# RWKV-5 attention with a SwiGLU block on one core: state update in 32-column groups, and another order of the opening

## The chip, the cores and the metric

The kernel runs on one core of a Trainium2 chip. The metric is device time in microseconds, the median over runs of the same program; lower is better. Timelines count from the start of the profiled span.

## The reference

Inputs are r, k and v of shape (4, 8, 768, 48) (batch, heads, tokens, head width D), w and u of shape (8, 48), and three float32 weights: `w_gate` and `w_val` of 384x1536, `w_out` of 1536x384. First the attention with a decaying state, then the FFN on all 3072 tokens:

```python
for t in range(S):
    kt, vt, rt = k[:, :, t], v[:, :, t], r[:, :, t]
    cur = einsum('bhd,bhe->bhde', u[None] * kt, vt)
    y[:, :, t] = einsum('bhd,bhde->bhe', rt, state + cur)
    state = w[None, :, :, None] * state + einsum('bhd,bhe->bhde', kt, vt)
x = y.transpose(0, 2, 1, 3).reshape(B * S, H * D)
g = x @ w_gate
out = (g * (1 / (1 + exp(-g))) * (x @ w_val)) @ w_out
```

All values are float32.

## The kernel before

**Units.** A unit is one chunk of 128 tokens of one batch entry; there are 24, numbered with the batch innermost, so that unit i is batch i mod 4 and chunk i div 4, and units 0 to 3 have no earlier state. For a unit, `load` fetches k and r (token on the partitions) and `load_v` fetches v. `own_product` (POOL, two multiplies into `rk`) and `own_sum` (DVE, a reduction into `du`) make the product of a token with itself. `scale_k` and `scale_r` (POOL) multiply k and r by powers of w, giving `khat` and `rhat` in slots of the tile `hats`; `turn` transposes them on PE (`tp`) into `kT` and `rT`. For units 0 and 1 the raw k and r are transposed and multiplied by tables of powers (`pw`, `pv`) on DVE as they leave PSUM; from unit 2 on the scaled ones are transposed and copied out by ACT. From unit 12 (`BLOCKS`) DMA and DVE transpose instead.

`diagonal` writes `du` on the diagonal of the 128x128 score tiles `At` (eight heads, two buffers), by ACT one head at a time or by one multiply on POOL or DVE for several heads. `scores` makes kT against rT on PE (`s_ps`), and DVE's `copy_predicated` writes it above the diagonal, half of the heads at a time. `outputs` makes y in 32-column groups on PE: a matmul writes 32 of the 128 PSUM partitions, four groups beside each other; its terms are scores times v and state times r. ACT copies y to `xT`.

**State.** `Z[b]` holds, for each pair of heads, a 112x96 tile in which the two 48x48 blocks on the diagonal are states. `update` adds a unit: one matmul per pair gives both heads against both, and a multiply with `wL`, which is zero off the two blocks, discards the cross terms:

```python
dve.tensor_add(z[0:R2], ps[0:R2], z[0:R2])
pool.tensor_mul(z[0:R2], z[0:R2], w)
```

Units 20 to 23 have no update. `wL` is made from `own`, a mask of two columns, early in the program.

**Weights.** 18 blocks (`chunks`) of 768 elements per partition arrive as pairs of 32-bit words in three buffers and are rounded: ACT makes `w_mag` from the upper words (in two halves, in two PSUM banks) and `w_low` from the lower ones, DVE puts sign and magnitude together (two operations a half, `round_dve`), and POOL adds the low part (`round_pool`). `round_act` does ACT's and DVE's share of a block and starts later loads, `round_weights` does a POOL add for the block ahead and then `round_act`. Four weight sums for `w_out` follow on POOL.

**FFN.** For units 0 to 3, `gate_value` makes a feature block of 128 columns for a pair of units: six matmuls into `gv`, a sigmoid, two DVE multiplies. It stands in a list, `todo`, with the number of rounded blocks that it needs; `feed(n)` takes the first entries that are ready by program order. Later units go in fours (`four`, `project`) with fewer products, spread over the steps in the same way.

**Order.** Each engine runs its instructions in the order in which the program issues them (a schedule by hand), and DMA starts go through SP's queue in order. The opening is written out call by call; then a loop over steps s from 4 calls `own_sum`, `scale`, `own_product`, loads, `turn`, `scores(s - 1)`, `outputs(s - 2)` and `update(s - 2)`, with `gaps(s, n)` between them: each takes a weights step ("R") or an FFN piece ("F") from a table up to step 11, and a share of `todo` after that. From step 12 (`LATE`) on, `outputs` stands right behind `scores`. `warm(n)` puts matmuls of the identity with no use of the result into PE's queue.

Of the kernel before, what the change touches and what calls it, by code (L numbers as in the profile page):

```python
# [15 lines left out]
P = 128  # L16
# [6 lines left out]
def fast(  # L23
# [50 lines left out]
    rscale = cst.tile([P, H, D], FP32, name="rscale")  # L74
    own = cst.tile([P, 2], FP32, name="own")
    wL = cst.tile([P, HP, 2, D], FP32, name="wL")
    w128 = cst.tile([P, HP], FP32, name="w128")
# [29 lines left out]
    def raw(i):  # L107

        if i < 2:
            return khat[i][:, :, 0:D], rhat[i][:, :, 0:D]  # L110
        return k_ld[i % 2][:], r_ld[i % 2][:]
# [57 lines left out]

    def round_act(next_load=1):  # L170
        n = next_chunk("act")
        if n is not None:
            mags[n] = []
            lows[n] = two.tile([P, WN], INT32, name="w_low", tag="w_low")
            for hi, (ps, tag) in zip(halves(bits[n][:, :, 1], n), ((ps_w, "w_mag"), (ps_o, "o"))):
                mag = ps.tile([P, WN // 2], INT32, name="w_mag", tag=tag)
                mags[n].append(mag[:].rearrange("p (c f) -> p c f", c=hi.shape[1]))
                act.activation(  # L178
                    mags[n][-1].bitcast(FP32), hi.bitcast(FP32), AF.Abs, scale=float(2.0**-112)
                )  # L180
                if len(mags[n]) == 1:
                    act.activation(
                        lows[n][:], bits[n][:, :, 0].bitcast(UINT32), AF.Copy, scale=float(2.0**-29)
                    )
                    round_dve(n, 0)
            round_dve(n, 1)
            del bits[n]
            for _ in range(next_load):
                load_weights()

    def round_dve(n, half):
        hi = halves(bits[n][:, :, 1], n)[half]
        f = hi.shape[2]
        dst = chunks[n][1].bitcast(INT32)
        dst = dst[:, :, half * f : half * f + f] if hi.shape[1] == 3 else dst[:, half : half + 1]
        dve.tensor_scalar(dst, hi, -(1 << 31), None, ALU.bitwise_and)  # L196
        dve.scalar_tensor_tensor(  # L197
            dst, mags[n][half], 3, dst, ALU.logical_shift_left, ALU.bitwise_or
        )

    def round_pool():
        n = next_chunk("pool")
        if n is not None:
            del mags[n]
            dst = chunks[n][1].bitcast(INT32)
            low = lows.pop(n)[:].rearrange("p (c f) -> p c f", c=dst.shape[1])
            pool.tensor_tensor(dst, dst, low, ALU.add)
# [8 lines left out]
    def own_product(i):  # L216
        kl, rl = raw(i)
        if i == 1:

            rk = At[1][:, 0:3, :].rearrange("p x t -> p (x t)").rearrange("p (h d) -> p h d", h=H)  # L220
        else:
            rk = one.tile([P, H, D], FP32, name="rk", tag="rk")[:]
        pool.tensor_mul(rk, rl, kl)
        pool.tensor_mul(rk, rk, ub[:])
        rks[i] = rk
# [9 lines left out]
    dve.memset(hats[:, 0:6, :, D:64], 0.0)  # L235
    dve.memset(wcol[:], 1.0)
    for e in range(2):
        sp.dma_start(out=wcol[64 * e : 64 * e + D, :], in_=w.rearrange("(a e) d -> e d a", e=2)[e])
# [13 lines left out]
    def warm(n):  # L252

        ps = ps_f.tile([P, 2, 2 * P], FP32, name="warm", tag="gv")
        for _ in range(n):
            pe.matmul(ps[:, 0, 0:P], ident[:], ident[:], start=True, stop=True)

    warm(18)

    pool.memset(own[:], 1.0)  # L260
    for step, base in ((-64, 0), (64, D - 1)):
        pool.affine_select(
            out=own[:], in_=own[:], compare_op=ALU.is_ge, fill=0.0,
            base=base, pattern=[[step, 2]], channel_multiplier=1 if step < 0 else -1,
        )

# [48 lines left out]
    def diagonal(i):  # L315

        du = dus.pop(i)
        on_act = (HP, 0, H)[min(i, 2)]
        small.extend(
            lambda h=h: act.activation(  # L320
                At[i % 2][:, h, :], ident[:], AF.Identity, scale=du[:, h : h + 1]
            )
            for h in range(on_act)
        )
        if on_act < H:
            n = H - on_act
            (pool if i else dve).tensor_mul(
                At[i][:, on_act:H], ident[:].unsqueeze(1).to_broadcast([P, n, P]),
                du[:, on_act:H].unsqueeze(2).to_broadcast([P, n, P]),
            )  # L330
# [4 lines left out]
    def turn(i):  # L335
        for nm, t, table in (
            ("kT", khat[i % 4], pw[:, :, 1 : P + 1]), ("rT", rhat_of(i), pv)
        ):
            tp = ps_a.tile([P, HP, P], FP32, name="tp", tag="a")
            for a in range(HP):  # L340
                pe.transpose(tp[:, a, :], pair(t, a), ident[:])
            if nm == "kT":
                dst = kT[i % 2]
            else:
                dst = turned[i] = three.tile([P, HP, P], FP32, name=nm, tag=nm)
            if i < 2:
                dve.tensor_mul(dst[:], tp[:], table)
# [71 lines left out]
    def update(i):  # L419
# [3 lines left out]
        kh, vl, z = khat[i % 4], v_ld[i % 4], Z[b]  # L423
        ps = ps_a.tile([P, HP, D2], FP32, name="u_ps", tag="a")
        for a in range(HP):
            pe.matmul(  # L426
                ps[0:R2, a, :].rearrange("p (e d) -> p e d", e=2),
                pair(kh, a)[:, 0:R2],
                bass.AP(
                    tensor=vl.tensor, offset=vl[:, a, 0:1].offset,  # L430
                    ap=[list(vl[:].ap[0]), [64, 2], [1, D]],
                ),
                start=True, stop=True, skip_group_check=True,
            )
        w = wL[0:R2].rearrange("p a e d -> p a (e d)")
        if c == 0:
            dve.tensor_mul(z[0:R2], ps[0:R2], w)
        else:
            dve.tensor_add(z[0:R2], ps[0:R2], z[0:R2])
            pool.tensor_mul(z[0:R2], z[0:R2], w)  # L440

# [245 lines left out]
    def queue(g):  # L687
        if g == 0:
            todo.extend(
                (2 * f2 + 2, lambda j=j, f=f: gate_value(j, f))  # L690
                for f2 in range(FC // 2) for j in range(2) for f in (2 * f2, 2 * f2 + 1)
# [32 lines left out]
    EARLY[4] = ("R", "F", "", "F", "F")  # L724


    turn(0)
    natural_tables()
    own_sum(0)
    diagonal(0)  # L730
    own_product(1)
    load(2)
    load_v(2)
    load_weights()
    load(3)
    load_v(3)
    warm(3)
    turn(1)
    while small:
        small.popleft()()  # L740
    own_sum(1)
    scale_k(0)
    diagonal(1)
    scores(0)
    round_act(0)
    scores(1)
    warm(3)
    scale_k(1)
    outputs(0)
    round_pool()  # L750
    round_act()
    scale(2)
    outputs(1)
    round_pool()
    dve.tensor_copy(w128[:].unsqueeze(2), pw[:, :, 0:1])
    dve.tensor_mul(
        wL[:], w128[:].unsqueeze(2).unsqueeze(3).to_broadcast([P, HP, 2, D]),
        own[:].unsqueeze(1).unsqueeze(3).to_broadcast([P, HP, 2, D]),
    )

    dve.tensor_tensor(bad[:], held[:], wcol[:], ALU.not_equal)
    dve.tensor_reduce(badc[:], bad[:], axis=AX.X, op=ALU.add)
    dve.memset(ones[:], 1.0)

    own_product(2)
    scale(3)
    warm(4)
    queue(0)
    round_act(2)
    load(4)  # L770
    turn(2)
    own_product(3)
    update(0)
    update(1)
    own_sum(2)
    diagonal(2)
    feed(1, 8)
    turn(3)
    round_act(0)
    own_sum(3)  # L780
    scores(2)
    round_pool()
    load_v(4)
    load(5)
    feed(1)
    diagonal(3)
    while small:
        small.popleft()()
    scores(3)
    outputs(2)  # L790
    update(2)
    round_pool()
    scale(4)
    outputs(3)
    load_weights()
    update(3)
    round_act()
    own_product(4)
    load(6)
    feed(2)  # L800
    own_sum(4)
    round_weights()
    for s in range(4, N + 2):
# [11 lines left out]
        if 4 <= s - 1 < N:  # L815
# [3 lines left out]
            if s >= LATE:  # L819
                outputs(s - 2)  # L820
            gaps(s, 1)
        if BLOCKS <= s < N:
# [4 lines left out]
        if s - 2 >= 4 and (s < LATE or s > N):  # L827
            outputs(s - 2)
        if s >= 5 and s % 2:
            queue((s - 3) // 2)  # L830
        if s < N:
            diagonal(s)
        if s - 2 >= 4:
            gaps(s, 3)
            update(s - 2)
        gaps(s, 4)
        if s == 12:
            n_ps = ps_a.tile([P, HP, P], FP32, name="n_ps", tag="a")
            pe.matmul(n_ps[0:1, 0, 0:1], badc[:], ones[:], start=True, stop=True)
# [418 lines left out]
```

## Time and profile before

| | |
|---|---|
| median of three runs | 640.49 us (639.94 to 641.51) |
| profiled execution | 640.14 us, span 638.3 us |
| TensorE clock granted, mean | 0.995 |
| busy: PE / DVE / POOL / ACT | 624.0 / 367.4 / 299.1 / 242.0 us |
| DMA | 40.40 MB, mean 63 GB/s |
| PE, state update (`u_ps`) | 160 records for 80 matmuls |
| DVE, state (L437, L439) | 4 and 16 operations, median 552 and 557 ns |
| POOL, state (L440) | 16 operations, median 1000 ns |

A matmul is pipelined, so that its recorded duration is longer than the time until the next one can start: the distance between starts is its price when PE is full. A float32 matmul leaves two records. The weight loads of the array have a row of their own (PEld) and run beside matmuls. A row of a timeline has its start, its length, the engine, the line, the operation, and the tiles written and read; in brackets stands the engine's idle time before it and what ended that.

### The profile page before, as it was taken

What the parts mean: (1) busy time and instruction counts of PE and PEld (TensorE: products, weight loads), DVE (VectorE), ACT (ScalarE), POOL (GpSimd) and SP (SyncE); (2) the same over time, 40 slices, a digit from 0 to 9 for tenths busy, and PEclk for the clock granted to TensorE, in tenths of its full rate; (3) what the DMA queues carried; (4) which work ended last, traced back from release to release, by engine and by line L of the source; (5) the groups of instructions that cost most, each with busy time, mean ns of one, the idle gap of its engine ahead of it and who ended that gap; (6) DMA issues with size and microseconds to landing.
All of it is one profiled execution on the core that took longest, in us unless ns stands there. A gap on an engine that the chain in (4) does not pass through costs nothing.

```text
span 638.3 us, 11992 instructions
## 1 busy us (share of the span) xinstructions
PE 624.0 (98%) x4570; PEld 561.6 (88%) x4570; DVE 367.4 (58%) x729; ACT 242.0 (38%) x655; POOL 299.1 (47%) x330
## 2 busy tenths in 40 slices
PE   8889999999999999999999999999999999999996
PEld 8678888899888889988899988889988889988896
DVE  7859998455356565366558255666255545355460
ACT  3558776421343421244431234442243320234310
POOL 5868877934837431754534734631432311444110
PEclk9989999999999999999999999999999999999998
DMA  8969873233322113212221402021100000000001
GB/s 197 263 161 232 223 213 89 40 65 73 79 48 37 33 26 71 66 32 52 45 47 31 109 5 46 16 40 27 51 1 2 1 1 26 26 1 1 2 2 53
DMA packets 138003, 40.40 MB, mean 63 GB/s; under 512 B 128592, under 2 KB 131792, under 8 KB 137936
## 3 DMA queue, kind: packets, MB, share of 16 engines
q1 hardware_dynamic: 134480, 34.82, 24.8%
q10 hardware_dynamic: 3456, 4.72, 2.1%
q8 instruction: 38, 0.62, 0.4%
q14 instruction: 29, 0.24, 0.1%
HBM read 28.51 MB, written 4.72 MB: 52 GB/s over the span
## 4 chain that ended last, share of the span: by engine, by line
PE 85%; DVE 8%; ACT 3%; POOL 1%; issue 1%; DMA 0%; SPq 0%; DVEq 0%; ACTq 0%
PE c_b L628 24%; PE c_a L628 20%; PE o_f L522 13%; PE o_a L522 8%; PE o_b L522 6%; PE y_ps L413 5%; PE gv L451 4%; PE s_ps L383 3%; PE u_ps L426 2%; ACT At L320 1%; DVE wg L196 1%; DVE At L388 1%; DVE wv L196 1%; ACT w_mag L178 1%; DVE wv L197 1%
## 5 line engine op out<-in xcount | busy, mean ns | idle before, releaser
L612 POOL TENSOR_TENSOR hT<-hT,u 128x256 f32<-128x256 f32 x60 | 47.5, 792 | 161.2 <-DVE hT L611 134.2
L635 ACT COPY u<-c_a 128x256 f32<-128x256 f32 x120 | 44.5, 371 | 86.9 <-PE c_a L628 85.6
L628 PE MATMUL c_a<-t,wv 128*128 128x256 f32 x240 | 72.2, 382 | 0.1
L628 PE MATMUL c_b<-xT,wg 128*128 128x256 f32 x240 | 71.7, 380 | 0.0
L608 ACT ACTIVATE sg<-hT 128x256 f32<-128x256 f32 x120 | 50.0, 416 | 54.2 <-DVE hT L637 35.5
L320 ACT ACTIVATE At<-ident,du 128x128 f32<-128x128 f32 x180 | 63.0, 398 | 12.5 <-DVE o_sb L536 7.8
L628 PE MATMUL c_b<-xT,s 128*128 128x256 f32 x240 | 61.6, 379 | 0.0
L642 DVE TENSOR_TENSOR u<-u,c_b 128x256 f32<-128x256 f32 x60 | 25.1, 418 | 62.1 <-PE c_b L628 55.1
L628 PEld LDWEIGHTS c_b<-xT,s 128*128 128x128 f32 x240 | 45.3, 190 | 6.6 <-DVE u L642 0.2
L628 PEld LDWEIGHTS c_a<-t,wv 128*128 128x128 f32 x240 | 44.7, 190 | 7.0 <-ACT u L635 1.1
L628 PEld LDWEIGHTS c_b<-xT,wg 128*128 128x128 f32 x240 | 45.2, 190 | 6.2 <-issue 0.4
L588 POOL TENSOR_TENSOR s<-wv,wg 128x256 f32<-128x256 f32 x24 | 17.8, 741 | 69.8 <-PE o_f L522 55.3
L637 DVE TENSOR_TENSOR hT<-p,c_b 128x256 f32<-128x256 f32 x60 | 25.2, 419 | 43.5 <-PE c_b L628 40.0
L388 DVE COPY_PREDICATED At<-mask,s_ps 128x512 f32<-128x512 int32 x48 | 32.8, 739 | 18.1 <-PE s_ps L383 10.8
L413 PE MATMUL y_ps<-At,v_ld 128*32 128x128 f32 x768 | 36.1, 279 | 4.7 <-DVE At L388 4.7
L451 PE MATMUL gv<-xT,wg 128*128 128x256 f32 x144 | 36.8, 391 | 0.0
L644 DVE TENSOR_TENSOR hT<-u,c_b 128x256 f32<-128x256 f32 x60 | 25.2, 421 | 19.4 <-PE c_b L628 19.2
L413 PEld LDWEIGHTS y_ps<-At,v_ld 128*32 128x32 f32 x768 | 30.9, 112 | 6.1 <-DVE At L388 5.7
L628 PE MATMUL c_b<-t,s 128*128 128x256 f32 x120 | 36.2, 383 | 0.0
L640 DVE TENSOR_TENSOR hT<-hT,c_a 128x256 f32<-128x256 f32 x60 | 25.3, 421 | 18.9 <-PE c_a L628 17.5
L628 PE MATMUL c_b<-xT,wv 128*128 128x256 f32 x120 | 35.9, 381 | 0.0
L628 PE MATMUL c_a<-xT,wg 128*128 128x256 f32 x120 | 35.8, 380 | 0.0
(139 smaller groups left out, 1411.7 us busy)
## 6 DMA issues: line engine op xcount, KB each, us to landing
hats<-hats SPq DMA_DIRECT2D x192, 32.0 KB, 1.9
w_bits<-in_moe_w_gate_dram SPq DMA_DIRECT2D x6, 768.0 KB, 5.9
v_ld<-in_v_dram SPq DMA_DIRECT2D x48, 96.0 KB, 3.0
w_bits<-in_moe_w_val_dram SPq DMA_DIRECT2D x6, 768.0 KB, 5.8
w_bits<-in_moe_w_out_dram SPq DMA_DIRECT2D x6, 768.0 KB, 5.1
out_dram<-o_sb ACTq DMA_DIRECT2D x24, 192.0 KB, 1.9
k_ld<-in_k_dram SPq DMA_DIRECT2D x22, 192.0 KB, 2.8
r_ld<-in_r_dram SPq DMA_DIRECT2D x22, 192.0 KB, 3.7
```

Of the source, the lines that this page charges most:

```text
L320: lambda h=h: act.activation(At[i % 2][:, h, :], ident[:], AF.Identity, scale=du[:, h : h + 1])
L388: dve.copy_predicated(At[i % 2][:].rearrange("p (a e) t -> p a e t", e=2)[:, :, e], mask[:].bitcast(INT32).unsqueeze(1).to_broadcast([P, H ...
L413: pe.matmul(ps[32 * q : 32 * q + 32, cc, :], *x, start=start, stop=stop, skip_group_check=True,)
L451: pe.matmul(gv[:, o, :].rearrange("p (i t) -> p i t", i=2), wt[:, c, P * f : P * (f + 1)], xT[:, 2 * g % NX : 2 * g % NX + 2, c, :], start ...
L522: pe.matmul(ps, lhs[:, f, :], rhs[:, f, :], start=(f == 0 and n in (0, 1, 4)), stop=(f == FH - 1), skip_group_check=True,)
L608: act.activation(x[what, f][:], h[j], AF.Sigmoid)
L612: pool.tensor_mul(h[1], h[1], x.pop(("u3", f))[:])
L628: pe.matmul(ps.rearrange("p (i t) -> p i t", i=2), lhs, rhs, start=first, stop=what not in ("p2", "p5", "p4", "p3"), skip_group_check=True,)
L635: act.copy(x[nm, f][:], ps)
L637: dve.tensor_add(h[0], x.pop(("p1", f))[:], ps)
L640: dve.tensor_mul(h[0], h[0], ps)
L644: dve.tensor_add(h[1], x.pop(("u2", f))[:], ps)
```

## The change

**State.** `update` makes each head's state alone, in 32-column groups: sixteen matmuls of 32x48 for a unit, two groups for a head (the columns from 48 on are zeros), of which the groups of both heads of a pair lie beside each other in PSUM. Two DVE operations and two POOL operations of 48x192 follow, with `w128` spread over the columns; `own` and `wL` are gone, and `Z` is set to zero at the start. In the loop `update` stands directly behind `outputs`.

**Units 2 and 3.** They are transposed unscaled, as units 0 and 1 are, and multiplied on DVE. Their loads go into `hats`, so that the r load of unit 2 or 3 replaces that of unit 0 or 1. `scale_k` comes later. The diagonals of units 0 to 3 are half on ACT and half on POOL.

**Weights and features.** The first two blocks are rounded by halves in an order of their own, with POOL adds by halves (`add_low`). The first feature needs no whole block and comes before the other halves.

**Order.** The opening is written anew; the check of w's range (`bad`, `badc`) moves to step 12.

```diff
-        if i < 2:
-            return khat[i][:, :, 0:D], rhat[i][:, :, 0:D]
+        if i < 4:
+            return khat[i][:, :, 0:D], rhat[i % 2][:, :, 0:D]
...
+    def add_low(n, half):
+
+        dst = chunks[n][1].bitcast(INT32)
+        f = dst.shape[2] // 2
+        cols = slice(half * f, half * f + f)
+        low = lows[n][:].rearrange("p (c f) -> p c f", c=dst.shape[1])
+        pool.tensor_tensor(dst[:, :, cols], dst[:, :, cols], low[:, :, cols], ALU.add)
...
+    for z in Z:
+        pool.memset(z[:], 0.0)
...
-        on_act = (HP, 0, H)[min(i, 2)]
+        on_act = HP if i < 4 else H
...
-            if i < 2:
+            if i < 4:
                 dve.tensor_mul(dst[:], tp[:], table)
...
-        ps = ps_a.tile([P, HP, D2], FP32, name="u_ps", tag="a")
+        ps = ps_a.tile([P, HP, D], FP32, name="u_ps", tag="a")
         for a in range(HP):
-            pe.matmul(
-                ps[0:R2, a, :].rearrange("p (e d) -> p e d", e=2),
-                pair(kh, a)[:, 0:R2],
-                bass.AP(
-                    tensor=vl.tensor, offset=vl[:, a, 0:1].offset,
-                    ap=[list(vl[:].ap[0]), [64, 2], [1, D]],
-                ),
-                start=True, stop=True, skip_group_check=True,
-            )
-        w = wL[0:R2].rearrange("p a e d -> p a (e d)")
-        if c == 0:
-            dve.tensor_mul(z[0:R2], ps[0:R2], w)
-        else:
-            dve.tensor_add(z[0:R2], ps[0:R2], z[0:R2])
-            pool.tensor_mul(z[0:R2], z[0:R2], w)
+            for q in range(4):
+                e, half = divmod(q, 2)
+                pe.matmul(
+                    ps[32 * q : 32 * q + 32, a, :], kh[:, 2 * a + e, 32 * half : 32 * half + 32],
+                    vl[:, a, 64 * e : 64 * e + D],
+                    start=True, stop=True, skip_group_check=True,
+                )
+        for e in range(2):
+            rows = slice(64 * e, 64 * e + D)
+            ze = z[rows, :, D * e : D * e + D]
+            w = w128[rows].unsqueeze(2).to_broadcast([D, HP, D])
+            if c == 0:
+                dve.tensor_mul(ze, ps[rows], w)
+            else:
+                dve.tensor_add(ze, ps[rows], ze)
+                pool.tensor_mul(ze, ze, w)
```

The new opening, in the order of its calls (`flush` issues the diagonal's ACT operations):

```python
turn(0); natural_tables(); own_sum(0); diagonal(0); flush(); own_product(1)
load(2); load_weights(); load_v(2); warm(3); turn(1); load(3); load_v(3)
scores(0); own_sum(1); diagonal(1); round_high(0, 0, 0); round_low(0); flush()
round_dve(0, 0); scores(1); warm(2); scale_k(0); add_low(0, 0); outputs(0)
round_high(1, 0, 1); round_low(1); round_dve(1, 0); add_low(1, 0)
own_product(2); scale_k(1); outputs(1); queue(0)
for n in range(2):
    round_high(n, 1, n); round_dve(n, 1); add_low(n, 1)
load_weights(); turn(2); feed(1); own_sum(2); diagonal(2); flush(); own_product(3); turn(3)
scores(2); update(0); update(1); own_sum(3); diagonal(3); flush(); scores(3)
scale_k(2); outputs(2); load(4); round_act(); feed(1); outputs(3); scale_k(3)
round_act(); round_pool(); scale(4); load_v(4); feed(1); update(2); update(3)
round_pool(); own_product(4); load(5); feed(1); own_sum(4); round_act(); load(6)
```

## The prediction

> **What bounds the kernel now.** I read the page first, then busy time by stretch, then the timeline of PE around the edited instructions, then POOL's and DVE's timelines up to 50 us.
>
> ```profile
> PE 624.0 (98%) x4570; PEld 561.6 (88%) x4570; DVE 367.4 (58%) x729; ACT 242.0 (38%) x655; POOL 299.1 (47%) x330
> ```
>
> ```profile
> 0.00:8.00 8.00, 6.58 (x35) 6.58 (x36) 4.19 (x19) 1.49 (x2) 2.18 (x12) 1.00 0.55 101
> 8.00:30.00 22.00, 18.52 (x205) 15.76 (x204) 21.23 (x35) 10.68 (x24) 18.77 (x16) 1.00 1.04 269
> 30.00:47.30 17.30, 14.88 (x135) 12.32 (x134) 9.37 (x19) 9.85 (x27) 11.23 (x10) 0.90 0.65 171
> 47.30:106.00 58.70, 57.22 (x537) 48.96 (x536) 54.96 (x95) 46.26 (x109) 45.85 (x38) 1.00 0.74 199
> 106.00:638.30 532.30, 526.76 (x3667) 478.02 (x3665) 277.64 (x564) 173.71 (x496) 221.06 (x258) 1.00 0.17 36
> ```
>
> Columns: stretch, its length, busy PE, PEld, DVE, ACT, POOL, granted clock, DMA share, GB/s. There are three regimes. From 106 us on PE alone is full: time taken off PE comes off the end. From 47 to 106 us (weights rounded) DVE is 94% busy and PE 97%: two near-equal bounds, so a gain on PE alone is not paid out. Before 47 us PE is partly idle or on warm-up matmuls; between 30 and 47 us DVE too is idle for 8 us.
>
> ```profile
> 394.01 0.59 PE L628 MATMUL c_a<-t,s 128*128 128x256 f32 x2
> 394.44 0.94 PE L426 MATMUL u_ps<-v_ld,hats 128*112 128x96 f32 x8
> 395.21 0.62 PE L628 MATMUL c_b<-t,s 128*128 128x256 f32 x2
> 395.67 0.60 PE L628 MATMUL c_b<-xT,wv 128*128 128x256 f32 x2
> ```
>
> ```profile
> 371.54 0.27 PE L413 MATMUL y_ps<-rT,Z 112*32 112x128 f32 x1
> 371.55 0.27 PE L413 MATMUL y_ps<-At,v_ld 128*32 128x128 f32 x1
> 371.55 0.37 PE L413 MATMUL y_ps<-rT,Z 112*32 112x128 f32 x3
> 371.65 0.27 PE L413 MATMUL y_ps<-At,v_ld 128*32 128x128 f32 x1
> ```
>
> A matmul leaves two records (two passes). The old state update is eight records; the next matmul starts 0.77 us later and its own slot is 0.46 instead of 0.43, so an update costs PE 0.80 us, 0.10 a pass. y's 32-column groups start almost together (371.54, 371.55, 371.55) and the next four 0.11 us later: four groups run side by side, each taking 0.107 us a pass of 128 columns.
>
> ```profile
> 39.60 1.00 POOL L224 TENSOR_TENSOR rk<-rk,ub 128x384 f32<-128x384 f32 x1
> 44.69 1.82 POOL L207 TENSOR_TENSOR wg<-wg,w_low 128x768 int32<-128x768 int32 x1 [4.09 <-DVE wg L197]
> ```
>
> ```profile
> 42.06 0.56 DVE L437 TENSOR_TENSOR Z<-u_ps,wL 112x384 f32<-112x384 f32 x1 [2.36 <-PE u_ps L426]
> 42.54 0.42 DVE L196 TENSOR_SCALAR wg<-w_bits 128x384 int32<-128x384 int32 x1
> ...
> 48.94 0.41 DVE L196 TENSOR_SCALAR wv<-w_bits 128x384 int32<-128x384 int32 x1
> ```
>
> This is the hole in the opening: POOL waits 4.09 us for DVE, DVE 2.36 us for PE's late update of unit 3, and the fifth weights block (42.54) waits behind that.
>
> **State in 32-column groups.** Sixteen matmuls of 32x48 replace four of 112x96: 32 records for 8. Stream: 128 columns take 0.107 us, so 48 take 0.040; with y's 0.003 of slack 0.043. Each group makes 8 passes, four groups at once: 8 x 0.043 = 0.34, with an edge 0.37 us. Weight loads of 32 columns (0.11 against 0.178 us recorded for 112) hide behind streaming in y. No mode change is added: the update joins y, whose exit (last y start 372.42, next full slot) is paid already. Saving 0.80 - 0.37 = 0.43 us.
>
> No row has a 48-column pass. [...] The third bound is y's mean pace, 0.11/4 per record: 32 x 0.0275 = 0.88, 0.08 lost. [...]
>
> The vector side: one DVE op of 112x384 (pitch 0.47 for two behind each other: 27.55, 1.01 for two) becomes two of 48x192. [...] 2 x 0.27 = 0.54, +0.07 us. POOL: 1.0 us becomes about 2 x 0.6 (768 int take 1.83, 384 take 1.0), +0.2; it has room after 106 us. On DVE the adds now stand right behind the two copies of the scores. In the step at 370 us the copies end at 372.62; y ends near 372.7, u would end near 373.1, so DVE waits 0.6 us (PE's write included), adds until 373.8, and only then runs the FFN multiply that ran at 372.51. Its next wait for PE lasted 1.43 us (till 374.35): that covers it. If the cover is gone, see the second rival.
>
> **Start.** Four memsets of Z enter POOL ahead of the identity. 128x128 takes 0.20, 128x2 0.10; so 128x384 about 0.41, pitched 0.35: 1.4 us later. The three `own` operations (0.55 us) go, but stood behind the identity. The 18 warm-up matmuls start 1.4 later: 26 of 36 records took 1.40 to 7.00 (0.215 each), the rest 0.11 each. If the pace doubles at 7.0 again, six or seven records move from the slow to the fast pace, and PE is free 0.7 us later. [...] I take 0.7 (kT at 9.4 instead of 8.83).
>
> **Opening, in the order of the new program.** Durations are the rows of before. DVE loses wL (2.19), bad (0.96, now at step 12), its half of At 0 (1.28); it gains four turned multiplies (0.6 each) in place of four ACT copies. POOL loses two rscale multiplies (1.0 each) and half of At 1 (0.96); it gains halves of At 0, 2, 3 (1.0 each).
>
> - rk0 ends 9.8 on POOL, du0 11.15, At 0's half 12.15; rk1, behind it in POOL's queue, 14.5; du1 15.25; At 1 at 16.5; copies of unit 1 16.5 to 17.8 (before 17.48 to 18.8); y1 ends 18.9.
> - POOL: scale_k 17.25, first half add 18.2, second (DVE ready 19.3) 20.25. The first feature runs 20.3 to 22.9 on PE (before 23.6 to 26.4). POOL: rk2 22.5, scale_k 23.5, two half adds 25.3, At 2 26.3, rk3 28.5, At 3 30.4, scale_k of 2 and 3 32.4.
> - SP: the r loads of 2 and 3 now wait for turn 0 and 1 (9.8, 12.2) and own products (8.4, 13.2): past before they were issued anyway (12.60, 18.57). r(3) still lands at 24.0. Block 3 waits for block 0's second half (20.8; before issued 22.6). Block 5 waits for block 2's rounding: issue about 34 against 27, with v(4) and unit 5 queued behind it; landing near 40, first used at 41.6.
> - PE: turn 3 at 24.0 to 24.8, scores 2, states 0 and 1, copies 26.3 to 27.6, y2 28.5, feature 31.2, y3 32.6 (before 41), feature, states, feature: 38.8. Before, the same four features ended at 47.25: PE is 8.4 us ahead.
> - POOL and DVE after that: add of block 2 35.7, scale(4) 37.7, block 3 39.6, rk4 41.6. Then du4 42.1, block 4 to 44.6, block 5 to 46.8; before block 5 ended at 51.0: DVE 4.2 ahead. POOL has scale(5), rk5 and block 4 done at 47.4, before 51.16: 3.8 ahead.
>
> So the fixed amount passes POOL and DVE 3.8 us earlier, although PE is further ahead: the stage to 106 us is theirs. Three Z adds there cost 3 x 0.07. Gain at 106 us: 3.6 us. The updates of units 4 to 6 save PE time only where DVE rules: counted as nothing.
>
> **Sum.** From 106 us on, the updates of units 7 to 19: 13 x 0.43 = 5.6. With 3.6: 9.2. The profiled execution took 640.14 (span 638.3 and 1.8 around it), 0.35 under the median of 640.49. 640.14 - 9.2 = 630.9; against the median 631.3.
>
> **Rivals.**
> 1. Narrow passes don't overlap (0.80 to 0.88 an update): only the opening pays, 640.5 - 3.6 + (0 to 1.0) = about 637. [...] Against: y's simultaneous starts.
> 2. DVE parked behind the state. If an FFN product needs DVE within the 1.1 us that it stands still and adds (0.6 + 0.54), PE stalls that long at each of 16 updates: 18 us lost, less 9.2, about 649. It decides from 9.2/16 = 0.6 us of stall a step. For: DVE already waited 8.3 us in 9 waits on this product, and c_b is reused after three slots (1.3 us). Against: the list of PE's waits shows none for DVE after 106 us, and the 1.43 us above.
> 3. The opening pays nothing, because POOL's queue (diagonal halves ahead of own products) eats it: 640.5 - 5.6 = 635. For: rk4 ends at 41.6, before at 40.6. Against: the hole of 4.09 behind it.
> 4. PE's lead of 8.4 us is paid out in full, DVE having less contention with POOL (its L196 took 0.41 to 2.2 us): 626.5.
>
> **Numbers.** Main case 0.56, first rival 0.11, second 0.10, third 0.14, fourth 0.09. A run of this kernel tells 0.3% (1.9 us) from no change. The second rival is nearly all slower, and a bad opening beside rival 1 is the 0.06 of no change: faster 0.84, same 0.06, slower 0.10. The range leaves out rival 2 and the outer parts of rivals 1 and 4: 626.5 to 638.
>
> **What would show it.** u_ps as 32 records a unit, under 0.45 us from y's last group to the next FFN slot (right), or 0.8 (rival 1). PE with no idle before L628 from 143 us on (rival 2 if c_b rows show DVE). Fourth feature over near 39 us and block 5's DVE rounding near 47 (opening); the last rounding near 102 instead of 106. Were the time above 639, both terms would be wrong.

## The result and the profile after

The changed kernel takes 629.51 us (median of six runs, 628.68 to 629.79) against 640.57 us for the kernel before on the same chip: ratio 0.983, 95% interval 0.981 to 0.9843. The prediction said 631.3. Its profiled execution has a span of 627.9 us against 638.3, so the two traces differ by 10.4 us.

The engines' line of the page:

```profile
PE 611.4 (97%) x5040; PEld 550.5 (88%) x5040; DVE 366.8 (58%) x751; ACT 239.5 (38%) x647; POOL 300.1 (48%) x350
```

PE is busy 12.6 us less, with 470 more records; DVE, ACT and POOL are within 2.5 us of where they were. Busy time by stretch (columns as in the prediction):

```profile
30.00:47.30 17.30, 16.70 (x209) 13.97 (x208) 14.23 (x29) 10.89 (x23) 14.15 (x13) 1.00 0.73 183
47.30:106.00 58.70, 55.19 (x624) 46.91 (x622) 54.28 (x100) 44.97 (x109) 47.98 (x41) 1.00 0.78 213
106.00:627.90 521.90, 516.07 (x3924) 469.09 (x3922) 275.85 (x574) 172.70 (x492) 218.24 (x269) 1.00 0.18 35
```

The hole from 30 to 47 us is filled: DVE 14.2 us busy there instead of 9.4, POOL 14.2 instead of 11.2. From 47 to 106 us PE has more slack than it had (55.2 of 58.7 us busy, before 57.2). A late step, PE first, then DVE:

```profile
362.93 0.40 PE L411 MATMUL y_ps<-At,v_ld 128*32 128x128 f32 x8
363.15 0.52 PE L426 MATMUL u_ps<-v_ld,hats 128*32 128x48 f32 x32
363.61 0.70 PE L627 MATMUL c_b<-xT,wg 128*128 128x256 f32 x2
```

```profile
361.76 1.38 DVE L386 COPY_PREDICATED At<-mask,s_ps 128x512 f32<-128x512 int32 x2 [0.73 <-PE s_ps L381]
363.77 0.74 DVE L438 TENSOR_TENSOR Z<-u_ps,Z 48x192 f32<-48x192 f32 x2 [0.64 <-PE u_ps L426]
364.55 0.44 DVE L610 TENSOR_TENSOR hT<-hT,sg 128x256 f32<-128x256 f32 x1
365.21 0.42 DVE L636 TENSOR_TENSOR hT<-p,c_b 128x256 f32<-128x256 f32 x1 [0.22 <-PE c_b L627]
```

The same place in the kernel before, where no state stands between:

```profile
372.42 0.40 PE L413 MATMUL y_ps<-At,v_ld 128*32 128x128 f32 x8
372.75 0.70 PE L628 MATMUL c_b<-xT,wg 128*128 128x256 f32 x2
```

From y's last eight records to the next FFN slot 0.68 us pass after the change and 0.33 before. The 32 records of the new state thus cost 0.35 us. DVE stands 0.64 us before the state's adds, and has nothing late behind them: it waits for PE again at 365.21.

Where the 10.4 us arise can be read from the same event in both traces. DVE's copies of the scores of unit 8, before and after:

```profile
106.25 1.36 DVE L388 COPY_PREDICATED At<-mask,s_ps 128x512 f32<-128x512 int32 x2
100.67 1.35 DVE L386 COPY_PREDICATED At<-mask,s_ps 128x512 f32<-128x512 int32 x2
```

That is 5.6 us ahead; at the copies of unit 4 the lead was 4.6 (55.36 to 50.78). From unit 8 on the lead of y grows by 0.46 us at most units: 5.59 us at unit 8, 6.05 at unit 9, 10.41 from unit 20. Before unit 4 the opening made the lead, after unit 8 PE's own time; how the lead grew between 50 and 106 us is what the experiments had to find out.

Part of the lead at unit 4 is the clock's. In the profile of the kernel before the granted clock is at half from 37.7 to 41.1 us; in that of the change it stays at 1.00 up to 624.9 us, behind PE's last record. The 32 records of one unit's y, before in that stretch and after:

```profile
39.04 1.94 PE L413 MATMUL y_ps<-At,v_ld 128*32 128x128 f32 x32
33.82 1.08 PE L411 MATMUL y_ps<-At,v_ld 128*32 128x128 f32 x32
```

Half clock for 3.4 us takes about 1.7 us from PE (an estimate), and the wait in the prediction's hole, 2.36 us of DVE for PE's update of unit 3, lies in it and just behind it (39.7 to 42.1 us). So the new order of calls made as little as 2.9 of the 4.6 us. Of the 64 timed runs of the kernel before on the experiments' chips, the eight with a granted clock of at least 0.999 took 639.2 us on average, the others 640.4. Whether the fuller opening itself keeps the clock up was not separated.

### The profile page after: what moved, and what is told of

It is laid out like the page before. It is cut to its first block, busy times and chain, and to the rows that moved or that the text cites. A ratio compares the mean times of both kernels' runs of the same rounds, so it can differ in the third digit from the quotient of the medians.

```text
span 627.9 us, 13037 instructions
## 1 busy us (share of the span) xinstructions
PE 611.4 (97%) x5040; PEld 550.5 (88%) x5040; DVE 366.8 (58%) x751; ACT 239.5 (38%) x647; POOL 300.1 (48%) x350
## 4 chain that ended last, share of the span: by engine, by line
PE 86%; DVE 7%; ACT 2%; DMA 2%; issue 1%; POOL 0%; DVEq 0%; ACTq 0%; POOLq 0%
PE c_b L627 25%; PE c_a L627 21%; PE o_f L521 13%; PE o_a L521 8%; PE o_b L521 6%; PE y_ps L411 5%; PE gv L450 4%; PE s_ps L381 3%; DVE At L386 1%; PE warm L265 1%; DMA hats<-in_r_dram 1%; DMA w_bits<-in_moe_w_out_dram 1%; DVE wg L188 1%; DVE wo L188 1%; PE u_ps L426 1%
## 5 line engine op out<-in xcount | busy, mean ns | idle before, releaser
L304 POOL TENSOR_TENSOR hats<-r_ld,rscale 128x384 f32<-128x384 f32 x20 | 20.9, 1045 | 36.1 <-DMA v_ld<-in_v_dram 19.0
L627 PE MATMUL c_a<-t,s 128*128 128x256 f32 x120 | 35.8, 380 | 0.0
```

What stands on the lines that cost most here:

```text
L627: pe.matmul(ps.rearrange("p (i t) -> p i t", i=2), lhs, rhs, start=first, stop=what not in ("p2", "p5", "p4", "p3"), skip_group_check=True,)
```

## The experiments

Ratios are to the kernel before on the same chip, with 95% intervals; spans are of the profiled executions.

### The two halves of the change

**State alone.** The kernel before with the new `update` behind `outputs`, `Z` zeroed, no `own` and `wL`; the opening as it was.

```diff
             outputs(s - 2)
+            update(s - 2)
...
             gaps(s, 3)
-            update(s - 2)
```

> The kernel before with the state part alone: 32-column groups behind y, Z zeroed on POOL behind the mask, no own and wL; opening and rounding order as before. Theory A (an update costs PE 0.35 us against 0.80, paid only where PE rules, from unit 7 on): 13 x 0.45 = 5.9 us, up to 1 us lost to single waits, and up to 1 us from the wL multiply (2.19 us) that DVE drops before 24 us: ratio 0.990 to 0.993, about 635. Rival B (the saving is paid at all 20 updates): 9 us, ratio 0.986. Rival C (DVE parked behind the state stalls PE): ratio above 0.995.

Measured: 631.28 us, 0.985 (0.9833 to 0.9866), span 629.8, 8.5 less than before. The number is B's. In the trace 1.7 us are there at the copies of unit 4 (wL's 2.19 us on DVE are gone), 3.55 at those of unit 8, and 8.5 at the end. The granted clock of this trace averages 0.92 from 8 to 30 us and 0.90 from 30 to 47 us.

**Opening alone.** The changed kernel with the old 112x96 matmuls at the old place.

```diff
-                update(s - 2)
...
             gaps(s, 3)
+            update(s - 2)
```

> The changed kernel with the old four matmuls of 112x96 a unit at their old place in the loop (vector operations of 48x192 kept, the cross terms not read): the opening's share alone. Theory A (the parts add up; the opening gave 5.6 us by 106 us in the trace): ratio 0.991, about 635; with e1 the two gains add to 11 within 1 us. Rival B (the narrow updates were needed for the opening's gain, since PE sits between 47 and 106 us at 97%): gain below 4 us, ratio above 0.994.

Measured: 638.21 us, 0.9977 (0.9965 to 0.9989), span 635.8. It is 4.0 us ahead at the copies of unit 4, 3.1 at those of unit 8, and 2.5 at the end: B's number, though not for B's reason, as the fillers below show. The granted clock of this trace is 1.00 in every stretch, so a part of its lead at unit 4 is the clock's, as above. The medians are the fairer measure: 9.0 and 2.0 us, 11.0 together against 11.1 for the whole, though both contain the loss of wL.

### Where PE's price of the state comes from

**State at its old place.** The changed kernel with `update` back behind `gaps(s, 3)`, between full-array matmuls.

```diff
-                update(s - 2)
             gaps(s, 1)
...
             gaps(s, 3)
+            update(s - 2)
```

> The changed kernel with the narrow update back at its old place, between full-array FFN matmuls: what the place behind y is worth. Theory A (a switch from full array to 32-column groups and back costs what y's exit shows, 0.33 us from y's last start to the next FFN slot where 0.11 is streaming, so some 0.2 us): 13 updates x 0.2 = 2.6 us, up to 4 us with the entry counted: ratio against before 0.987 to 0.989. Rival B (no switch cost in the middle): as the changed kernel, 0.983. Rival C (DVE's waits for the state vanish and win time): below 0.982.

Measured: 637.51 us, 0.9952 (0.9936 to 0.9969), span 634.7: 6.8 us longer than the change's, of which 4.4 come from unit 8 on and most of the rest between the copies of units 5 and 8 (the table below). That is more than any of the three theories had, A's 4 us included. PE around one update:

```profile
390.65 0.59 PE L627 MATMUL c_a<-t,s 128*128 128x256 f32 x2
391.18 0.55 PE L426 MATMUL u_ps<-v_ld,hats 128*32 128x48 f32 x32
391.66 0.70 PE L627 MATMUL c_b<-t,s 128*128 128x256 f32 x2
392.19 0.59 PE L627 MATMUL c_b<-xT,wv 128*128 128x256 f32 x2
```

c_a's start to the state 0.53, the state to c_b 0.48, c_b's own slot 0.53: 1.54 us, where two undisturbed slots take 0.86 (0.43 each). So 0.68 us an update against 0.35 behind y: about half of an update's price between full-array matmuls is going into column groups and out again. Behind y that is paid already. Against the old form's 0.80 the narrow matmuls alone would bring 0.12 us an update.

**Groups one after another.** The same 16 matmuls with the loops exchanged, so that the four of one group are issued behind each other.

```diff
-        for a in range(HP):
-            for q in range(4):
+        for q in range(4):
+            for a in range(HP):
```

> The changed kernel with the 16 matmuls of an update in another order: all four pairs of one column group, then the next group, so that neighbours share a group. Theory A (the saving is four groups side by side; PE starts in program order, so that a group's 8 passes of 0.0425 us block the next group's): an update takes 32 x 0.0425 = 1.36 us instead of 0.35: 13 x 1.0 = 13 us slower than the changed kernel and up to 5 more before 106 us, ratio 1.003 to 1.01. Rival B (starts are not bound to program order across groups): no change, 0.983.

Measured: 638.09 us, 0.9967 (0.9956 to 0.9978), span 636.0.

```profile
370.20 1.10 PE L426 MATMUL u_ps<-v_ld,hats 128*32 128x48 f32 x32
371.24 0.70 PE L627 MATMUL c_b<-xT,wg 128*128 128x256 f32 x2
```

1.04 us from the state's first record to the next slot instead of 0.46: 0.58 more for the same 32 records. The price lies between the two theories. 32 passes of 0.0425 us one after another, and the 0.12 us that 0.46 has over eight of them, would be 1.48 us; the 0.44 less are some 0.15 us, three to four passes, by which a group starts ahead of the end of the one before (an estimate). That the four groups run side by side, which the first rival denied, is shown; so is that it depends on their order. From unit 9 to unit 21 the copies of this kernel fall behind the change's by these 0.58 us at almost every unit.

### Which engine sets the pace between 47 and 106 us

The state alone had gained 1.9 us between the copies of units 4 and 8, where the prediction let PE's time count as nothing. Two kernels with the same extra time, one on PE and one on DVE, both on the kernel before:

```diff
-        for a in range(HP):
+        for a in [a for a in range(HP) for _ in range(2 if 4 <= i < 9 else 1)]:
```

> The kernel before, with the scores matmuls of units 4 to 8 issued twice (16 records of 48x128 more in each of the steps 5 to 9, about 1.0 us of PE by their rows, 1.16 and 0.94 us; 5.0 us together; no other engine gets anything). Theory A, PE binds between 47 and 106 us (as the state alone, which was paid at every update, suggests): the time rises by 4 to 5.5 us, ratio 1.006 to 1.0085. Theory B, the prediction's step, DVE binds there and PE's time counts as nothing: under 1.5 us, ratio below 1.0025.

```diff
-        dve.tensor_scalar(dst, hi, -(1 << 31), None, ALU.bitwise_and)
+        for _ in range(2 if 5 <= n < 17 and half == 0 else 1):
+            dve.tensor_scalar(dst, hi, -(1 << 31), None, ALU.bitwise_and)
```

> The kernel before, with DVE's sign operation (0.35 to 0.42 us, undisturbed) issued twice for the first half of each of the weights blocks 5 to 16: twelve more, 4.8 us of DVE between 47 and 100 us, nothing more for PE. Theory A, PE binds: most is absorbed, under 2 us, ratio below 1.003. Theory B, DVE binds: 4 us or more, ratio above 1.006. Should both this kernel and the one with doubled scores rise by 3 us or more, the two engines wait for each other in turn and neither alone binds.

Measured: with PE's filler 642.59 us, 1.0038 (1.0024 to 1.0051); with DVE's 648.56 us, 1.0136 (1.012 to 1.0153). DVE's is theory B's number; PE's lies between the two theories (A from 1.006, B below 1.0025), and the traces have to decide. Of PE's filler, the copies of two steps and the doubled matmuls before the second:

```profile
106.80 1.35 DVE L388 COPY_PREDICATED At<-mask,s_ps 128x512 f32<-128x512 int32 x2
115.96 1.36 DVE L388 COPY_PREDICATED At<-mask,s_ps 128x512 f32<-128x512 int32 x2 [0.79 <-ACT At L320]
```

```profile
47.30:106.00 58.70, 58.70 (x578) 51.15 (x580) 54.55 (x94) 46.00 (x108) 45.93 (x37) 1.00 0.76 203
100.68 2.06 PE L383 MATMUL s_ps<-rT,kT 48*128 48x128 f32 x32
```

PE got 4.5 us more (2.06 instead of 1.16 in each of five steps) and fills the stretch to the last hundredth, yet unit 8's copies come 0.55 us late (106.80 for 106.25), and those of unit 3, before the first filler, were already 0.63 late (38.02 for 37.39). Only at the next copies, with the rounding over, does the backlog show: 2.0 us (115.96 for 113.92). DVE's twelve fillers made unit 8's copies 7.8 us late (114.02); 0.9 of that was there at unit 3, before the first of them, and the remaining 6.9 are more than their own 4.8 us:

```profile
90.43 3.22 DVE L197 TENSOR_SCALAR wo<-w_bits 128x384 int32<-128x384 int32 x2
114.02 1.36 DVE L389 COPY_PREDICATED At<-mask,s_ps 128x512 f32<-128x512 int32 x2
```

So DVE sets the pace there, as the prediction had it, and PE has some 2.5 us of slack over the stretch (4.5 less the backlog); what exceeds the slack is paid later. Then what did the state gain there? The line above points to it: two sign operations of 0.35 us took 3.22.

### Sign operations beside POOL

A third theory (C in the expectations): the state moves POOL's operations, and with them the time that DVE's sign operations lie beside them. POOL and DVE of the kernel before in one step, then of the state alone:

```profile
99.35 1.05 POOL L440 TENSOR_TENSOR Z<-Z,wL 112x384 f32<-112x384 f32 x1 [3.14 <-DVE Z L439]
100.36 1.82 POOL L207 TENSOR_TENSOR wo<-wo,w_low 128x768 int32<-128x768 int32 x1
```

```profile
99.19 0.35 DVE L196 TENSOR_SCALAR wo<-w_bits 128x384 int32<-128x384 int32 x1
100.12 2.28 DVE L196 TENSOR_SCALAR wo<-w_bits 128x384 int32<-128x384 int32 x1
102.51 0.56 DVE L197 SCALAR_TENSOR_TENSOR wo<-w_mag,wo 128x384 int32<-128x384 int32 x1
```

```profile
95.45 1.08 POOL L435 TENSOR_TENSOR Z<-Z,w 48x192 f32<-48x192 f32 x2 [2.14 <-DVE Z L434]
96.61 2.03 POOL L205 TENSOR_TENSOR wo<-wo,w_low 128x768 int32<-128x768 int32 x1
```

```profile
96.59 0.35 DVE L194 TENSOR_SCALAR wo<-w_bits 128x384 int32<-128x384 int32 x1
97.52 1.34 DVE L194 TENSOR_SCALAR wo<-w_bits 128x384 int32<-128x384 int32 x1
```

Before, the sign operation of 100.12 began under POOL's state multiply and ended at 102.40, when POOL's weights add (until 102.18) was over: 2.28 us for 0.35. With the state earlier, the weights add is already half done when that operation begins, and it costs 1.34. In the other order (96.59, just ahead of the add) the sign operation keeps its 0.35 us and the add takes 2.03 instead of 1.82. Both long ones end 0.22 us behind the weights add: the 1.34 at 98.86, the 2.28 at 102.40, although the multiply under which the 2.28 began was over at 100.40.

Two kernels take the theory apart. The old state, early in the steps up to 11 only:

```diff
+            if s < LATE:
+                update(s - 2)
...
-            update(s - 2)
+            if s >= LATE:
+                update(s - 2)
```

> The kernel before with its old state (112x96 matmuls, one DVE and one POOL operation), moved behind y in the steps up to 11 only (updates of units 4 to 9); the later steps are as they were. PE saves nothing. Theory C, formed from the traces: between 47 and 106 us DVE sets the pace, and its sign operation (0.35 to 0.41 us alone) lasts up to 2.28 us beside POOL's weights add, which starts when POOL's state multiply, late behind a late DVE add, is done; an earlier state starts POOL's adds about 1 us sooner and takes 0.9 us a step off those collisions. Then 2 to 3.5 us are gained, ratio 0.9945 to 0.997, and the summed excess of the long sign operations between the scores copies of units 5 and 8 falls from 9.9 us to near 7. Theory D, the gain of the state in these steps was PE's own time: no gain here, 0.999 to 1.001.

And the state alone (new matmuls behind y), with its DVE and POOL operations left behind `gaps(s, 3)` in those steps:

```diff
-            update(s - 2)
+            then = update(s - 2)
...
             gaps(s, 3)
+            if s < LATE:
+                then()
```

> The kernel before with the new state behind y, where in the steps up to 11 only the matmuls stand there and the state's DVE and POOL operations stay at their old place behind the FFN pieces. PE saves as much as with the whole state early. Theory C: what that version gained between the scores copies of units 5 and 8 (1.9 us, and 2.2 to 3 over all the steps to 11) goes: 633.5 to 635 us, ratio 0.990 to 0.9925. Theory D: as the whole state early, 631.3, ratio 0.984 to 0.987.

Measured: 640.74 us, 1.0008 (0.9996 to 1.002), and 633.74 us, 0.9898 (0.9884 to 0.9912). The second is C's number: with PE's saving complete, 2.5 us of the gain are gone once the adds come late. In the traces 0.7 us of that stand at the copies of unit 4 already, before the first add that was moved, and 1.9 come between those of units 4 and 8: there this kernel's lead does not grow (0.97 to 0.89 us), although PE saves as much. The first is D's number, against C: place alone brings nothing. Its trace says why:

```profile
99.07 1.01 POOL L440 TENSOR_TENSOR Z<-Z,wL 112x384 f32<-112x384 f32 x1 [1.43 <-DVE Z L439]
100.03 1.84 POOL L207 TENSOR_TENSOR wo<-wo,w_low 128x768 int32<-128x768 int32 x1
```

```profile
99.69 2.42 DVE L196 TENSOR_SCALAR wo<-w_bits 128x384 int32<-128x384 int32 x1
```

POOL's pair comes earlier, but so does the sign operation, again under the state multiply. The table sums the 18 sign operations between the copies of units 5 and 8, where DVE is idle for 2.2 to 2.7 us in all and the granted clock is 1.00 in all six traces:

| kernel | the 18 sign operations | copies of unit 5 to unit 8 |
|---|---|---|
| before | 16.94 us | 40.94 us |
| old state early | 17.03 us | 41.02 us |
| new matmuls early, adds late | 16.16 us | 41.05 us |
| state alone | 14.13 us | 39.06 us |
| change | 15.00 us | 40.27 us |
| change, state at the old place | 16.92 us | 42.17 us |

The last two rows differ by 1.92 and 1.90 us: the sign operations are the whole difference. The state alone has 2.81 us less of them than before and pays 0.44 for its two DVE operations a step; of the rest 1.88 arrives. So the gain of the state between 47 and 106 us is shown to be DVE's, not PE's, and to need early adds together with the new form: the form alone takes 0.78 us off the sign operations, the place alone nothing, both together 2.81.

What the form does can be read from the fourteen traces between 20 and 125 us. Fifteen sign operations begin under the old multiply of 112x384, and all fifteen wait through the weights add behind it too. Another 206 begin under some other POOL operation with the next one directly behind, nine of them under the new multiplies of 48x192, and every one ends 0.2 to 0.35 us after the operation under which it began (those that begin in its last 0.08 us are left out). The old state early keeps the old multiply, and so gains nothing. With the new form a late state still puts the start of the sign operation early into the add (1.9 us), an early one lets it begin halfway (1.34). Why the old multiply holds DVE over the next operation is open.

### Smaller parts of the opening

**One round more** in the changed kernel's opening, and **one round less** in the kernel before's:

```diff
     load(6)
+    round_weights()
     for s in range(4, N + 2):
```

> The changed kernel with one more weights step (POOL add of block 4, ACT and DVE rounding of block 5) ahead of the loop, as the kernel before has it. Theory A (the changed opening reaches 106 us by 5.6 us earlier, where the sum had 3.6, because it leaves one block of some 2.5 us of DVE time to step 10, where DVE has room): 2 to 2.5 us slower than the changed kernel, ratio against before 0.986 to 0.987. Rival B (where the block is rounded makes no difference, the opening itself gave all): 0.9826 as the changed kernel, within 0.5 us.

```diff
     own_sum(4)
-    round_weights()
     for s in range(4, N + 2):
```

> The kernel before without its last weights step ahead of the loop, so that every block from the sixth on comes one weights step later; nothing else changed. Theory A (DVE rules from 47 to 106 us, and a block moved behind that stretch is time won): 2 to 2.5 us faster than before, ratio 0.996. Rival B: no difference, or slower by up to 1 us because POOL's weight sums end later.

Measured: 635.78 us, 0.992 (0.9905 to 0.9935), 6.3 more than the change, of which its trace has 1.2 at the copies of unit 2, ahead of the added step; and 639.96 us, 0.9991 (0.998 to 1.0003), no difference. The first is worse than both theories. Its list of PE's waits:

```profile
PE tp L343 <- POOL hats L301: 3.7, 1, 3.7
```

The POOL add stands ahead of a scale that unit 5's transpose needs. Beside that wait, the granted clock averages 0.989 in this trace, against 0.998 in the change's; what that costs was not separated. The missing round of the opening is thus no gain by itself, and with one more the opening is slower.

**The adds later.** In the changed kernel, the state's DVE and POOL part behind `gaps(s, 1)` from step 12 on.

```diff
-                update(s - 2)
+                then = update(s - 2)
             gaps(s, 1)
+            if s >= LATE and then:
+                then()
```

> The changed kernel with DVE's and POOL's part of the state, from step 12 on, moved behind the FFN pieces that follow; PE's part stays behind y. Theory A (the single waits of PE after 143 us are chance collisions of DVE and POOL, not DVE parked behind the state): within 0.5 us of the changed kernel, ratio 0.982 to 0.9835. Rival B (the parked DVE costs): 0.7 to 1 us faster, ratio below 0.9815.

Measured: 633.2 us, 0.9882 (0.9865 to 0.99), 3.7 more than the change, against both theories. In the trace 1.1 us of it are there at the copies of unit 2, long before the edit acts, and 2.6 arise from step 12 on. PE now waits 1.5 us for `hT` in two places; the other 1.1 stand in no wait of the list. DVE's standing before the adds costs PE 0.3 us at most (its only late wait in the change); moving the adds costs more.

**Z's memsets behind the mask**, off the way of the identity.

```diff
-    for z in Z:
-        pool.memset(z[:], 0.0)
...
         base=0, pattern=[[1, P]], channel_multiplier=-1,
     )
+    for z in Z:
+        pool.memset(z[:], 0.0)
```

> The changed kernel with the four memsets of Z behind the mask on POOL instead of ahead of the identity. Theory A (the 0.7 us that PE's start is late is absorbed: y of unit 0 starts at 15.1 in both traces, as DMA and DVE set what follows): within 0.5 us of the changed kernel. Rival B (the late start runs through to 106 us): 0.7 us faster, ratio 0.9815.

Measured: 629.9 us, 0.983 (0.9815 to 0.9844), as the change. PE starts 0.6 us sooner, and waits for the landing of the loads instead. No version tried is faster than the change.

## Why the prediction was right, and where it was not

**An update's price: right.** 0.35 us measured, 0.37 predicted; passes of the four groups 0.0425 us apart, predicted 0.043. "No mode change is added" holds, and the state at its old place shows that it was the larger half of the saving: 0.33 of 0.45 us. The row of y before showed it: its four groups start within 0.02 us (371.54 to 371.56), and those of the state do so too (363.155 to 363.175). DVE's two operations were put too low, 0.54 us for 0.74 measured (363.77), which PE does not feel where it sets the pace. The 0.96 elements per ns in that estimate are the rate of DVE's rows in the kernel before, which take 0.355 us for 192 columns (L536) and 0.555 for 384 (L439); too low was the fixed part, 0.07 us, where 0.37 an operation leaves 0.17 (an estimate).

**Updates of units 7 to 19, predicted 5.6 us.** From unit 8 to unit 20 the lead grows by 4.8 us over twelve updates, 0.46 each where PE is full. The thirteenth, of unit 7, brings nothing (the lead is 5.58 us at the copies of unit 8 and 5.59 at those of unit 9). 12 x 0.46 would be 5.5; the missing 0.7 go at units 13 and 17. In this part the list of PE's waits has one for DVE (us, times, longest):

```profile
PE c_b L627 <- DVE hT L636: 0.3, 1, 0.3
```

That row is all that the second rival's mechanism (DVE parked) came to. DVE's predicted wait of 0.6 us is there, 0.64, and covered.

**The opening, predicted 3.6 us at 106 us.** Its single times were late: the fourth feature ended at 41.8 us (predicted 38.8), block 5's DVE rounding at 48.7 (46.8), POOL's add of block 4 at 49.6 (47.4):

```profile
47.75 1.88 POOL L218 TENSOR_TENSOR wg<-wg,w_low 128x768 int32<-128x768 int32 x1
```

The opening alone had 3.1 us at the copies of unit 8, but ends with 2.5: 0.6 is lost again after 106 us. Up to 1.7 of these are the half-clock stretch of the trace it is compared with, for which the prediction has no term although its row (0.90 from 30 to 47 us) showed it. The timed runs give the opening 2.0 us by the medians, 0.7 to 2.2 by the interval of the ratio: this term was too high.

**The step that failed.** "The updates of units 4 to 6 save PE time only where DVE rules: counted as nothing", with "three Z adds there cost 3 x 0.07". Its premise is right, as the two fillers show. But with 5.6 us of lead at 106 us and 3.1 of it from the opening, the state brought 2.5 us up to there (1.9 between the copies of units 4 and 8 when it stands alone) instead of costing 0.2. The term left out is on DVE's own chain: a sign operation that begins under POOL's old state multiply waits through the weights add behind it (2.28 us), and with the new state, placed early, it begins under the add and takes 1.34. The prediction had the row of it in its fourth rival ("its L196 took 0.41 to 2.2 us") and did not weigh it. That the sum came so near is in part luck: 3.6 + 5.6 = 9.2 predicted, 5.6 + 4.8 = 10.4 measured, where the first 5.6 is an opening put too high, a gain on DVE that was not foreseen, and a stretch of half clock.

**The other rivals.** The first (no overlap) is refuted by 0.35 us an update; no run shows its 0.80 for an update of narrow passes, which took 0.68 between full-array matmuls and 0.93 group by group (0.35 and 0.58). The third (the opening pays nothing) is refuted by the opening alone, narrowly: its interval ends at 0.9989. The fourth (PE's lead paid in full) falls with PE's filler and with the late adds.

## What to carry to other kernels

Put narrow column-group matmuls beside others of the same tiling: here an update cost 0.35 us there and 0.68 between full-array ones. Where DVE sets the pace, ask of every POOL instruction that a change moves or reshapes which DVE operations it will lie beside; a DVE row of one shape with durations from 0.35 to 2.4 us is the sign. A gain that has the expected size is no proof of its mechanism: the state alone matched theory B (9 us expected, 9.0 measured), and only fillers on both engines and the late adds showed that another engine had made 1.9 us of it. And read the clock's column in both traces before a lead is put down to the order of calls.

## What the runs showed of the hardware that was not expected

- A sign operation that begins under a POOL operation ends 0.2 to 0.35 us after it, even if the next one stands directly behind (206 of 206). Under the old multiply of 112x384 it waits through the next one too (15 of 15): at 100.12 us it began under a multiply that ended at 100.40, and ended behind the add that ran from 100.36 to 102.18.
- Going into column groups and back costs about 0.33 us between full-array matmuls (0.68 less 0.35); 16 matmuls issued group by group cost 0.58 us more than interleaved.
- The granted clock fell to half for 3.4 us in the trace of the kernel before (37.7 to 41.1 us). In the state alone it averages 0.92 from 8 to 30 us and 0.90 from 30 to 47, which at half clock is 22 x 0.08 / 0.5 = 3.5 us and 17.3 x 0.10 / 0.5 = 3.5 us (an estimate).
